# Start-up of an attention and gated-MLP kernel: the norm's scale on GpSimd, two tiles ahead, and the first Q and K loads ahead of the next weights

## The chip, the core and the metric

One core of one Trainium2 chip runs the kernel. The metric is the device time of one execution in microseconds (us). The engines are named as the profile names them: PE is TensorE (PEld is its loading of weights), DVE is VectorE, ACT is ScalarE, POOL is GpSimd and SP is SyncE, which issues most of the DMAs. An engine runs its instructions in the order in which they are written, and waits in that order too.

## What is computed

The reference, cut to what matters (S = 2048 tokens, D = 576, 32 heads of 18, 4608 hidden units, all f32):

```python
xn = layernorm(x)                                  # no gain, no bias
q, k, v = heads(xn @ wqkv)                         # 32 heads of 18
p = softmax(q @ k.T * 18 ** -0.5)                  # per head, 2048 x 2048
s = merge(p @ v) @ wo
h = gelu(xn @ w_gate) * (xn @ w_up)                # 2048 x 4608
return x + s * silu(h @ w_down)
```

The kernel holds every f32 operand of a matmul as two f16 parts, a high half and a low half (the rest), and multiplies high by high, high by low and low by high.

## The kernel before

**Order.** The function `tile_block_kernel` writes the program out in an order made by hand and by small planners. It has a start-up and a long main part. From about 220 us to the end the main part mixes the attention of all heads with the GLU matmuls, and its order is made by queues of pieces of work (`subtick`, `fill`, `g_run`) that are spent between matmuls.

**Norm.** `x` lies in SBUF as 16 tiles `xt[:, st]` of 128 tokens x 576. Per group of tiles `ln_stats` writes, on DVE, two `bn_stats` a tile (L1114) and one `bn_aggr` a tile (L1117), then for the group a square root on ACT (L1126), a reciprocal (L1127) and three small operations with two operands (L1120) that give the factor `rs_all`. The groups are tiles 0-1, 2-3, 4-7, 8-11 and 12-15. `ln_norm(st)` then subtracts the mean and multiplies by the factor, in place, on DVE (L1135, a `tensor_scalar` with two operands of one value per partition, `mv` and `rs_all`). ACT rounds to the high half `xn` (L1139), and POOL subtracts for the low half in two pieces, 64 columns (L1140) and 512 columns (L1141).

**Transposition and projection.** `ln_tr` puts nine 128x128 transpositions of a tile on PE (L1147) into a PSUM tile `tp`, and `ln_out` copies them on ACT to `XHT` (high, L1152) and `XL` (low, L1153). `proj_fine(st)` multiplies a tile by the Q and K weights of the first seven heads (28 matmuls, L412 to L415). After each fourth tile (a block of 512 tokens, `sb` 0 to 3) `evac_j` writes high and low halves of Q and K (ACT L514, DVE L519) and stores them to DRAM (L534), `QD` over POOL's DMA queue and `KD` over SP's. In the loop over `it` tile `it` is normalized, tile `it - 1` transposed, tile `it - 2` copied out and then projected.

**Weights.** `prep` makes one set of weights: the load (L229, L233, SP), row maxima (L248, DVE) and their exchange over DRAM (L274, L289, SP) for a common scale, a high half on ACT (L330) and a low half. The low half (`low`, L332) is one DVE instruction (L335) where `urgent` or `vec` is set, and two POOL instructions (L337 scale with one operand per partition, L338 subtract) elsewhere. `w0` are the Q and K weights of the first seven heads, `preps[0]` the V weights, whose pieces go into the loop by the table `V_PLAN` (iteration: pieces). After the loop `start_prep(1)` and `start_prep(2)` issue the loads of the Q and K weights of the next seven heads (`raw_j`) and line up the pieces of those and of GLU chunk 0 (`raw_c`).

**First scores.** Then `load_qk(0)` issues the loads of `KT` (L1242) and `QT` (L1243) of the first two heads from `KD` and `QD`, all on SP, and `fills(9, 2.0)` writes some 150 V matmuls (`unit_v`, L487 to L492, evacuated at L598 and stored to `VS` by POOL at L612). Only then come the first score matmuls `qk1(0, k)` (L1259), whose row maxima DVE takes (L1262, `PM`), two steps of `k` at a time between further V matmuls.

Of the kernel before, what the change touches and what calls it, by code (L numbers as in the profile page):

```python
# [31 lines left out]
V_PLAN = {8: 2, 9: 2, 10: 1, 11: 1, 12: 6, 13: 3, 14: 2, 15: 2, 16: 2, 17: 2}  # L32
# [62 lines left out]
def kernel(ctx: ExitStack, tc: tile.TileContext, x, wqkv, wo, w_gate, w_up, w_down, out):  # L95
# [114 lines left out]
    def prep(name, parts, n, down=None, urgent=False, free=None, dfree=None, lead=1, vec=()):  # L210
# [121 lines left out]
        def low(lo, raw, sc, hi, vec=False):  # L332

            if urgent or vec:
                nc.vector.scalar_tensor_tensor(lo, raw, sc, hi, op0=ALU.mult, op1=ALU.subtract)  # L335
            else:
                nc.gpsimd.tensor_scalar(raw, raw, sc, None, op0=ALU.mult)  # L337
                nc.gpsimd.tensor_tensor(lo, raw, hi, op=ALU.subtract)  # L338

        def split_lo(t):  # L340
            low(w.lo[:, t], w.raw[:, t], w.s[:, 0:1], w.hi[:, t], t in vec)
# [165 lines left out]
    def evac_j(j, part, sb, mt, n, late=None):  # L507
# [16 lines left out]
        def store():  # L524
# [7 lines left out]
            q = nc.gpsimd if j == 0 and part == 0 else nc.sync  # L532
# [459 lines left out]
    def start_prep(i):  # L992
        if i < len(order) and i not in preps:
# [4 lines left out]
                lead=2 if i == 3 else 1, vec=(1, 3) if i == 3 else (),  # L998
# [89 lines left out]
    w0, p0 = prep(*spec_j(0), urgent=True)  # L1088
# [44 lines left out]
    def ln_norm(st):  # L1133
        xs = xt[:, st]
        nc.vector.tensor_scalar(  # L1135
            xs, xs, mv[:, st, 0:1], rs_all[:, st:st + 1], op0=ALU.subtract, op1=ALU.mult
        )
        xn = xns[st] = ap.tile([P, 2 * D], F16, tag="P", name=f"xn{st}", bufs=6)
        nc.scalar.activation(xn[:, 0:D], xs, AF.Copy)  # L1139
        nc.gpsimd.tensor_tensor(xn[:, 576:640], xs[:, 512:576], xn[:, 512:576], op=ALU.subtract)  # L1140
        nc.gpsimd.tensor_tensor(xn[:, 640:1152], xs[:, 0:512], xn[:, 0:512], op=ALU.subtract)  # L1141

    def ln_tr(st):
        tp = tps[st] = ps.tile([P, 2, 1024], F16, tag=("s1", "s2")[st % 2], name=f"tp{st}")
        for i in range(9):
            b, c = divmod(i, 5)
            nc.tensor.transpose(tp[:, b, P * c:P * c + P], xns[st][:, P * i:P * i + P], ident)  # L1147

    def ln_out(st):
        sl = slice(P * st, P * st + P)  # L1150
        tp = tps[st]
        nc.scalar.activation(XHT[:, :, sl], tp[:, 0, 0:640].rearrange("p (a b) -> p a b", a=5), AF.Copy)  # L1152
        nc.scalar.activation(XL[:, :, sl], tp[:, 1, 0:512].rearrange("p (a b) -> p a b", a=4), AF.Copy)  # L1153
# [17 lines left out]
    with tc.manual_schedule():  # L1171
# [7 lines left out]
        s0, s1 = ln_stats(0, 2), ln_stats(2, 2)  # L1179
        for f in s0:  # L1180
            f()
        ln_norm(0)
        ln_norm(1)
        for f in s1[:3] + pw[:5]:
            f()
        ln_tr(0)
        ln_out(0)
        for f in pw[5:6] + s1[3:7] + pw[6:12] + s1[7:]:
            f()
        ln_norm(2)  # L1190
        pw[12]()
        ln_tr(1)
        ln_out(1)
        for f in pw[13:]:
            f()
        lnq = deque()
        for t in range(4, NT, 4):
            lnq.extend(ln_stats(t, 4))
        for _ in range(12):
            lnq.popleft()()  # L1200
        for it in range(2, NT + 2):
            g, i = divmod(it, 4)
            if 2 < it < NT:
                ln_norm(it)
            if g < 3:
                for _ in range((0, 0, 0, 5)[it] if it < 4 else (5, 4, 4, 4)[i]):
                    if lnq:
                        lnq.popleft()()
            if it == 5:
                open_j(w0, 0)  # L1210
            if it == 5:
                preps[0], pieces = prep(*order[0][1], urgent=True)
                pv0 = deque(f for _, f in pieces)
                pv0.popleft()()
            for _ in range(V_PLAN.get(it, 0)):
                pv0.popleft()()
            if it == 2:
                proj_fine(0)
            if it > 2:
                if it - 1 < NT:  # L1220
                    ln_tr(it - 1)
                if it - 2 > 1:
                    ln_out(it - 2)
                subtick()
                proj_fine(it - 2)
        while pv0:
            pv0.popleft()()
        start_prep(1)
        start_prep(2)
# [204 lines left out]
    load_qk(0)  # L1434
    fills(9, 2.0)
# [330 lines left out]
```

## Time and profile before

| what | us |
|---|---|
| median of the runs shown (2611.22 to 2614.23) | 2613.34 |
| the profiled execution's own time | 2613.96 |
| its span in the profile | 2612.2 |
| PE busy, share of the span | 2511.1, 96% |
| POOL busy, share of the span | 1507.7, 58% |

The profiled execution is 0.6 us above the median, and its span is 1.8 us shorter than its own time. Engines, their busy time and their share are in the page's first part; idle time of an engine that is not waited for costs nothing. The start-up is read by stages: a table of windows gives the busy time of each engine in each stretch, the granted TensorE clock and the DMA share, and the timelines of single engines give each instruction with the time it waited ahead of it, in brackets, and what ended the wait.

### The profile page before, as it was taken

To read this page: it belongs to the slowest core of one execution; us is meant where nothing else is said; L and a number is where in the kernel's file an instruction comes from. 1 tells how busy PE (TensorE), PEld (TensorE's weight loads), DVE (VectorE), ACT (ScalarE), POOL (GpSimd) and SP (SyncE) were. 2 spreads that over 40 slices of the span, in tenths; PEclk is the share of its full clock that TensorE was granted. 3 is DMA by queue.
4 is the path that set the end of the run, shared out by engine and by line. 5 is a ranking of instruction groups with operands and counts; after the bars stand their busy time and mean duration, and the time that the engine had idled before them with its cause. 6 is when DMAs were issued, how large, how long until landed. Compare 5 with 4: busy or idle time off the path is not lost. (4 is left out here: it accounts for less than half of the span.)

```text
span 2612.2 us, 60772 instructions
## 1 busy us (share of the span) xinstructions
PE 2511.1 (96%) x25800; PEld 1325.6 (51%) x25800; DVE 1931.7 (74%) x2713; ACT 1660.6 (64%) x2081; POOL 1507.7 (58%) x1426
## 2 busy tenths in 40 slices
PE   6899999999999999999999999999999999999997
PEld 5564545455545545455555455555445444445554
DVE  7587778777877777777777778777777777777544
ACT  5225666666767666766666666767666675766663
POOL 4247663576537553757656574847666675747412
PEclk9999999999999999999999999999999999999999
DMA  4431022202130112101011110201110111100123
GB/s 142 125 111 19 12 57 60 56 18 54 33 80 19 33 31 64 46 23 51 13 53 22 27 55 11 56 9 38 28 36 26 37 29 40 36 21 6 43 74 123
DMA packets 134156, 118.68 MB, mean 45 GB/s; under 512 B 60160, under 2 KB 112792, under 8 KB 133884
## 3 DMA queue, kind: packets, MB, share of 16 engines
q1 hardware_dynamic: 128892, 105.38, 15.2%
q0 software_dynamic: 2432, 6.54, 0.7%
q8 instruction: 201, 3.29, 0.5%
q10 hardware_dynamic: 2560, 2.89, 0.3%
q14 instruction: 71, 0.58, 0.1%
HBM read 84.89 MB, written 29.61 MB: 44 GB/s over the span
## 5 line engine op out<-in xcount | busy, mean ns | idle before, releaser
L1262 DVE TENSOR_REDUCE PM<-s 128x2 f32<-128x1024 f32 x1024 | 1250.9, 1224 | 341.5 <-PE s L1259 333.0
L1317 ACT ACTIVATE P<-s,etab 128x1024 f32<-128x1024 f32 x896 | 995.6, 1112 | 616.7 <-PE s L1311 601.1
L468 PE MATMUL ma_t<-XHT,whi_c 64*128 64x512 f16 x1440 | 542.9, 377 | 10.7 <-DVE osb L1342 5.6
L468 PE MATMUL mb_t<-XHT,whi_c 64*128 64x512 f16 x1440 | 542.9, 377 | 3.8 <-DVE touch L436 2.0
L468 PE MATMUL ma_t<-XHT,wlo_c 64*128 64x512 f16 x1296 | 488.5, 377 | 0.0
L468 PE MATMUL mb_t<-XHT,wlo_c 64*128 64x512 f16 x1152 | 434.1, 377 | 0.0
L468 PE MATMUL ma_t<-XL,whi_c 64*128 64x512 f16 x1152 | 433.8, 377 | 0.0
L468 PE MATMUL mb_t<-XL,whi_c 64*128 64x512 f16 x1152 | 433.7, 376 | 0.0
L1259 PE MATMUL s<-KT,QT 54*128 54x512 f16 x2048 | 399.5, 378 | 21.0 <-DMA QT<-QD 9.6
L1311 PE MATMUL s<-QT,KT 56*128 56x512 f16 x2048 | 406.0, 380 | 5.2 <-ACT P L1317 1.7
L468 PEld LDWEIGHTS <-whi_c 64*128 64x128 f16 x5184 | 276.8, 94 | 245.8 <-issue 30.4
L728 PE MATMUL md_t<-dhi_c,hhi 64*128 64x288 f16 x2304 | 341.7, 283 | 7.3 <-DVE osb L1344 2.3
L728 PE MATMUL md_t<-dhi_c,hlo 64*128 64x288 f16 x2304 | 341.4, 282 | 0.0
L728 PE MATMUL md_t<-dlo_c,hhi 64*128 64x288 f16 x2304 | 340.9, 282 | 0.0
L669 POOL TENSOR_SCALAR tw<-tw 128x512 f32<-128x512 f32 x144 | 90.9, 632 | 408.3 <-ACT tw L662 408.1
L728 PEld LDWEIGHTS <-hhi 64*128 64x128 f16 x4608 | 247.1, 94 | 141.4 <-issue 22.8
L1336 PE MATMUL md_t<-P,VT 128*32 128x512 f32 x2480 | 292.8, 596 | 0.7 <-ACT P L1317 0.5
L691 POOL TENSOR_TENSOR hlo<-gv,hhi 128x512 f16<-128x512 f32 x144 | 168.0, 1167 | 205.6 <-ACT hhi L684 194.9
L1311 PEld LDWEIGHTS <-KT 56*128 56x128 f16 x2048 | 126.0, 94 | 244.7 <-issue 158.4
L656 POOL TENSOR_TENSOR tw<-gs 128x512 f32<-128x512 f32 x144 | 150.6, 1046 | 140.1 <-ACT gs L633 139.7
L748 DVE SCALAR_TENSOR_TENSOR y<-md_t,c_c,y 128x576 f32<-128x576 f32 x272 | 219.2, 806 | 8.3 <-PE md_t L728 8.2
L468 PEld LDWEIGHTS <-wlo_c 64*128 64x128 f16 x2592 | 139.6, 94 | 122.1 <-issue 1.5
(249 smaller groups left out, 4067.2 us busy)
## 6 DMA issues: line engine op xcount, KB each, us to landing
draw_c<-in_B_w_down SPq DMA_DIRECT2D x18, 576.0 KB
raw_c<-in_B_w_gate SPq DMA_DIRECT2D x18, 512.0 KB
raw_c<-in_B_w_up SPq DMA_DIRECT2D x18, 512.0 KB
obr<-rd SPq DMA_DIRECT2D x30, 256.0 KB
KT<-KD SPq DMA_DIRECT2D x32, 224.0 KB
QT<-QD SPq DMA_DIRECT2D x32, 216.0 KB
VS<-vst POOLq DMA_DIRECT2D x16, 304.0 KB, 4.0
VT<-VS SPq DMA_DIRECT2D x16, 304.0 KB
```

What stands on the lines that cost most here:

```text
L468: nc.tensor.matmul(o, lw, xx, start=self.stage == 0 and self.k == 0, stop=self.stage == 1 and self.k == self.slots - 1, skip_group_check=True,
L656: gp.tensor_tensor(st["t"], st["g"], st["g"], op=ALU.mult)
L669: gp.tensor_scalar(st["t"], st["t"], 1.0, 1.0, op0=ALU.mult, op1=ALU.add)
L691: gp.tensor_tensor(hs.lo[:, ft], st["v"], hs.hi[:, ft], op=ALU.subtract)
L728: nc.tensor.matmul(self.t.t[:, hf, 0:288], a[r, ft, sl], b[r, ft, 288 * hf:288 * hf + 288], start=self.stage == 0 and k == 0, stop=self.st ...
L748: nc.vector.scalar_tensor_tensor(yy, y, w.c, yy, op0=ALU.mult, op1=ALU.add)
L1259: nc.tensor.matmul(s1[:, h], QT[p][r, P * qt:P * qt + P], KT[p][r, 512 * kb:512 * kb + 512], start=True, stop=True)
L1262: nc.vector.tensor_reduce(PM[p][:, :, qt, kb:kb + 1], s1, op=ALU.max, axis=AX.X)
L1311: nc.tensor.matmul(s2[:, h], KT[p][r, P * kt:P * kt + P], QT[p][r, 512 * qb:512 * qb + 512], start=True, stop=True)
L1317: nc.scalar.activation(pt, s2, AF.Exp, scale=ETAB[j0])
L1336: nc.tensor.matmul(t.t[qd:qd + 32, :], VT[p][:, c0:c0 + 32], pt[:, h], start=kt == k0, stop=kt == k1, skip_group_check=True,)
```

## The change

- **Scale on POOL.** `ln_norm` is split into `ln_scale` (the same `tensor_scalar`, now on GpSimd, L1135 of the new kernel), `ln_hi` (ACT, L1141) and `ln_lo` (one POOL instruction of 576 columns, L1145). In the loop at step `it` the scale of tile `it + 2` stands first, then the transpositions of tile `it`, the high half of `it + 1`, the copies of `it - 1`, the low half of `it + 1` and the projection of `it - 2`.
- **Statistics.** Groups are tiles 0-1, 2-3, 4-5, 6-7, 8-11 and 12-15, and they are written earlier.
- **Transpositions.** Ten a tile (L1151, L1153, L1155): four high, two of 64 columns, four low. The copies of the low half of tiles 9, 11, 13 and 15 go to DVE (L1163).
- **Weights.** The low halves 3 and 4 of `w0` go to POOL, 0 to 2 stay on DVE. Two of the low halves of each weight tile of GLU chunk 0 (`vec=(1, 3)`) go from POOL to DVE. `V_PLAN` spends the V pieces somewhat earlier.
- **Stores and loads.** The `QD` stores of the first three blocks go from POOL's to SP's queue. `start_prep(1)` and `start_prep(2)` stand behind `load_qk(0)`.

The order of PE's instructions from the seventh V matmul to the end is the same in both kernels (before, the first six stand between two projections), and so is that of the other engines from a little behind the first scores.

```diff
-V_PLAN = {8: 2, 9: 2, 10: 1, 11: 1, 12: 6, 13: 3, 14: 2, 15: 2, 16: 2, 17: 2}
+V_PLAN = {6: 2, 7: 2, 8: 1, 11: 1, 12: 6, 13: 3, 14: 3, 15: 3, 16: 2}
...
         def low(lo, raw, sc, hi, vec=False):
...
-            if urgent or vec:
+            if (urgent and vec is not None) or vec:
...
         def split_lo(t):
-            low(w.lo[:, t], w.raw[:, t], w.s[:, 0:1], w.hi[:, t], t in vec)
+            low(w.lo[:, t], w.raw[:, t], w.s[:, 0:1], w.hi[:, t], None if urgent and vec and t not in vec else t in vec)
...
-            q = nc.gpsimd if j == 0 and part == 0 else nc.sync
+            q = nc.gpsimd if j == 0 and part == 0 and sb == NB - 1 else nc.sync
...
-                lead=2 if i == 3 else 1, vec=(1, 3) if i == 3 else (),
+                lead=2 if i == 3 else 1, vec=(1, 3) if i in (2, 3) else (),
...
-    w0, p0 = prep(*spec_j(0), urgent=True)
+    w0, p0 = prep(*spec_j(0), urgent=True, vec=(0, 1, 2))
...
-    def ln_norm(st):
+    def ln_scale(st):
...
-        nc.vector.tensor_scalar(
+        nc.gpsimd.tensor_scalar(
...
-        xn = xns[st] = ap.tile([P, 2 * D], F16, tag="P", name=f"xn{st}", bufs=6)
-        nc.scalar.activation(xn[:, 0:D], xs, AF.Copy)
-        nc.gpsimd.tensor_tensor(xn[:, 576:640], xs[:, 512:576], xn[:, 512:576], op=ALU.subtract)
-        nc.gpsimd.tensor_tensor(xn[:, 640:1152], xs[:, 0:512], xn[:, 0:512], op=ALU.subtract)
+    def ln_hi(st):
+        xn = xns[st] = ap.tile([P, 2, D], F16, tag="P", name=f"xn{st}", bufs=6)
+        nc.scalar.activation(xn[:, 0], xt[:, st], AF.Copy)
+    def ln_lo(st):
+        xn = xns[st]
+        nc.gpsimd.tensor_tensor(xn[:, 1], xt[:, st], xn[:, 0], op=ALU.subtract)
...
     def ln_tr(st):
...
-        for i in range(9):
-            b, c = divmod(i, 5)
-            nc.tensor.transpose(tp[:, b, P * c:P * c + P], xns[st][:, P * i:P * i + P], ident)
+        xn = xns[st]
+        for c in range(4):
+            nc.tensor.transpose(tp[:, 0, P * c:P * c + P], xn[:, 0, P * c:P * c + P], ident)
+        for i in range(2):
+            nc.tensor.transpose(tp[64 * i:64 * i + 64, 0, 512:640], xn[:, i, 512:576], ident)
+        for c in range(4):
+            nc.tensor.transpose(tp[:, 1, P * c:P * c + P], xn[:, 1, P * c:P * c + P], ident)
...
     def ln_out(st):
...
+        lo = tp[:, 1, 0:512].rearrange("p (a b) -> p a b", a=4)
...
-        nc.scalar.activation(XL[:, :, sl], tp[:, 1, 0:512].rearrange("p (a b) -> p a b", a=4), AF.Copy)
+        if st >= 9 and st % 2:
+            nc.vector.tensor_copy(XL[:, :, sl], lo)
+        else:
+            nc.scalar.activation(XL[:, :, sl], lo, AF.Copy)
...
     def proj_fine(st):
...
+        early, late, high, low = pw[:5], pw[5:12], pw[12:13] + pw[13:20:2], pw[14:21:2] + pw[21:]
+        lnq = deque()
+        for t0, n in ((0, 2), (2, 2), (4, 2), (6, 2), (8, 4), (12, 4)):
+            lnq.append(deque(ln_stats(t0, n)))
+        def stats(n):
+            while n and lnq:
+                lnq[0].popleft()()
+                n -= 1
+                if not lnq[0]:
+                    lnq.popleft()
+        stats(11)
+        for t in range(2):
+            ln_scale(t)
+            ln_hi(t)
+        for t in range(2):
+            ln_lo(t)
+        stats(7)
+        for f in early[:4]:
...
+        stats(4)
+        early[4]()
...
+        for t in range(2, 4):
+            ln_scale(t)
+            ln_hi(t)
+        for t in range(2, 4):
+            ln_lo(t)
+        late[0]()
+        stats(3)
+        for f in late[1:]:
...
+        for f in high:
+            f()
+        stats(4)
+        for f in low[:3]:
+            f()
...
+        for f in low[3:]:
...
+        stats(4)
+        for t in range(4, 6):
+            ln_scale(t)
+        ln_hi(4)
         for it in range(2, NT + 2):
...
+            if it == 2:
...
+            stats(11 if it == 2 else 6)
+            if 5 < it + 2 < NT:
+                ln_scale(it + 2)
+            if it < NT:
+                ln_tr(it)
+            if 4 < it + 1 < NT:
+                ln_hi(it + 1)
+            if it - 1 < NT:
+                ln_out(it - 1)
+            if 3 < it + 1 < NT:
+                ln_lo(it + 1)
...
+            subtick()
+            proj_fine(it - 2)
...
-        start_prep(1)
-        start_prep(2)
...
+    start_prep(1)
+    start_prep(2)
```

**POOL, the norm loop.** The rows are of tiles 8 and 9 before, with the Q stores of the first block between them, and of tiles 0 to 7 in the new kernel. `xn_...` is the f16 tile of a norm tile, `evh` and `evl` the evacuated halves.

```order
L1140 TENSOR_TENSOR xn_530<-xt,xn_530 128x64
L1141 TENSOR_TENSOR xn_530<-xt,xn_530 128x512
L534 DMA QD_369<-evh_0_0_444 7x18x512 x2
L534 DMA QD_369<-evl_0_0_499 7x18x512
L1140 TENSOR_TENSOR xn_592<-xt,xn_592 128x64
L1141 TENSOR_TENSOR xn_592<-xt,xn_592 128x512
```

```order
L1145 TENSOR_TENSOR xn_171<-xt,xn_171 128x576
L1145 TENSOR_TENSOR xn_174<-xt,xn_174 128x576
L337 TENSOR_SCALAR raw_j_106<-raw_j_106,s_j_195 128x252
L338 TENSOR_TENSOR wlo_j_199<-raw_j_106,whi_j_198 128x252
L337 TENSOR_SCALAR raw_j_106<-raw_j_106,s_j_195 128x252
L338 TENSOR_TENSOR wlo_j_199<-raw_j_106,whi_j_198 128x252
L1135 TENSOR_SCALAR xt<-xt,mv,rs_all 128x576 x2
L1145 TENSOR_TENSOR xn_235<-xt,xn_235 128x576
L1135 TENSOR_SCALAR xt<-xt,mv,rs_all 128x576
L1145 TENSOR_TENSOR xn_374<-xt,xn_374 128x576
```

Before, POOL has one low half a tile and three stores a block; in the new kernel each tile brings a scale and a low half in turn, and two pairs of weight instructions stand ahead of tile 4.

**SP, the loads behind the norm loop.** `KD` and `QD` are the projected keys and queries in DRAM, `raw_j` the next weights, `mxd_j` their row maxima on the way to DRAM.

```order
L534 DMA KD_370<-evh_1_3_1052 7x18x512
L229 DMA raw_j_1066<-in_A_wqkv 128x4x126
L233 DMA raw_j_1066<-in_A_wqkv 128x1x126
L229 DMA raw_j_1066<-in_A_wqkv 128x4x126
L233 DMA raw_j_1066<-in_A_wqkv 128x1x126
L1242 DMA KT_1075<-KD_370 56x2048
L1243 DMA QT_1074<-QD_369 54x2048
L1242 DMA KT_1075<-KD_370 56x2048
L1243 DMA QT_1074<-QD_369 54x2048
L274 DMA mxd_j_1234<-mx_j_1232 128x1
```

```order
L534 DMA KD_238<-evh_1_3_1064 7x18x512
L1273 DMA KT_1082<-KD_238 56x2048
L1274 DMA QT_1081<-QD_237 54x2048
L1273 DMA KT_1082<-KD_238 56x2048
L1274 DMA QT_1081<-QD_237 54x2048
L229 DMA raw_j_1111<-in_A_wqkv 128x4x126
L233 DMA raw_j_1111<-in_A_wqkv 128x1x126
L229 DMA raw_j_1111<-in_A_wqkv 128x4x126
L233 DMA raw_j_1111<-in_A_wqkv 128x1x126
L274 DMA mxd_j_1320<-mx_j_1318 128x1
```

The four loads of the first two heads have passed the four loads of the next weights.

**DVE, the maxima behind the last evacuation.** `m_j` are the row maxima of the next weights, `PM` those of the scores `s`.

```order
L519 SCALAR_TENSOR_TENSOR evl_0_3_1058<-pv_t,evh_0_3_1054 126x512
L248 TENSOR_REDUCE m_j_1204<-raw_j_1066 128x1 x5
L262 TENSOR_REDUCE mx_j_1232<-m_j_1204 128x1
L1262 TENSOR_REDUCE PM_1080<-s_0_0_1276 128x2
L1262 TENSOR_REDUCE PM_1080<-s_0_1_1280 128x2
```

```order
L519 SCALAR_TENSOR_TENSOR evl_0_3_1070<-pv_t,evh_0_3_1066 126x512
L248 TENSOR_REDUCE m_j_1258<-raw_j_1111 128x1 x3
L1293 TENSOR_REDUCE PM_1087<-s_0_0_1282 128x2
L1293 TENSOR_REDUCE PM_1087<-s_0_1_1286 128x2
L248 TENSOR_REDUCE m_j_1258<-raw_j_1111 128x1 x2
L1293 TENSOR_REDUCE PM_1087<-s_0_2_1310 128x2
L1293 TENSOR_REDUCE PM_1087<-s_0_3_1314 128x2
L262 TENSOR_REDUCE mx_j_1318<-m_j_1258 128x1
```

Three of the five maxima of the next weights still stand ahead of the first row maxima, two come between them.

## Rows read from the trace of the kernel before

**Rows 1.** The page, first part: busy us (share of the span) and instructions of each engine.

```profile
PE 2511.1 (96%) x25800; PEld 1325.6 (51%) x25800; DVE 1931.7 (74%) x2713; ACT 1660.6 (64%) x2081; POOL 1507.7 (58%) x1426
```

**Rows 2.** Windows: stretch, its length, busy us of each engine (instructions), clock, DMA share.

```profile
core 0: us, PE busy (x) PEld busy (x) DVE busy (x) ACT busy (x) POOL busy (x), PEclk, DMA share, GB/s
24.00:62.00 38.00, 30.43 (x450) 28.42 (x448) 32.58 (x74) 27.54 (x50) 22.95 (x33) 0.96 0.25 74
...
85.00:95.00 10.00, 0.48 (x3) 0.20 (x4) 0.00 (x0) 0.00 (x0) 0.69 (x2) 0.69 0.21 44
95.00:100.00 5.00, 5.00 (x23) 2.34 (x24) 2.59 (x3) 0.41 (x1) 0.00 (x0) 0.60 0.55 120
100.00:105.00 5.00, 5.00 (x39) 3.16 (x37) 4.61 (x5) 0.82 (x2) 0.70 (x2) 1.00 0.44 138
```

**Rows 3.** PE's timeline: start us, us, operation, [idle before <-releaser].

```profile
67.52 0.29 PE L487 MATMUL ma_t<-whi_v,XHT 128*128 128x288 f16 x1
...
85.22 0.39 PE L1259 MATMUL s<-KT,QT 54*128 54x512 f16 x1 [0.27 <-DMA QT<-QD]
94.90 1.03 PE L1259 MATMUL s<-KT,QT 54*128 54x512 f16 x3 [9.29 <-DMA QT<-QD]
```

**Rows 4.** SP's timeline, issues of DMAs behind the norm loop.

```profile
70.00 0.96 SPq L229 DMA_DIRECT2D raw_j<-in_A_wqkv  x1
...
74.52 1.64 SPq L233 DMA_DIRECT2D raw_j<-in_A_wqkv  x1
76.34 2.06 SPq L1242 DMA_DIRECT2D KT<-KD  x1
...
79.38 0.47 SPq L1243 DMA_DIRECT2D QT<-QD  x1
```

**Rows 5.** DVE's timeline: the first scale, a small operation, the next weights' maxima, the first row maxima.

```profile
7.86 1.07 DVE L1135 TENSOR_SCALAR xt<-xt,mv,rs_all 128x576 f32<-128x576 f32 x2
...
25.95 1.08 DVE L1120 SCALAR_TENSOR_TENSOR nt<-mv,sd 128x4 f32<-128x4 f32 x1
27.06 0.16 DVE L1120 SCALAR_TENSOR_TENSOR nt<-nt,sd 128x4 f32<-128x4 f32 x1
...
81.94 1.38 DVE L248 TENSOR_REDUCE m_j<-raw_j 128x1 f32<-128x252 f32 x4 [12.90 <-DMA raw_j<-in_A_wqkv]
...
95.55 2.36 DVE L1262 TENSOR_REDUCE PM<-s 128x2 f32<-128x1024 f32 x2 [11.23 <-PE s L1259]
```

**Rows 6.** POOL's timeline: a low half, the last low half, the last Q stores.

```profile
25.86 1.15 POOL L1141 TENSOR_TENSOR xn<-xt,xn 128x512 f16<-128x512 f32 x1
...
60.80 1.15 POOL L1141 TENSOR_TENSOR xn<-xt,xn 128x512 f16<-128x512 f32 x1
...
69.98 0.61 POOL L534 DMA_DIRECT2D QD<-evl  x1
```

**Rows 7.** POOL's groups, whole run: xcount | busy us, mean ns | idle before.

```profile
L337 POOL TENSOR_SCALAR raw_c<-raw_c,s_c 128x512 f32<-128x512 f32 x88 | 139.3, 1583 | 60.8 <-ACT whi_c L330 51.9 <-PE s L1259 8.8
...
L669 POOL TENSOR_SCALAR tw<-tw 128x512 f32<-128x512 f32 x144 | 90.9, 632 | 408.3 <-ACT tw L662 408.1
...
L338 POOL TENSOR_TENSOR dlo_c<-draw_c,dhi_c 128x576 f16<-128x576 f32 x36 | 46.4, 1288 | 3.0
...
L337 POOL TENSOR_SCALAR raw_j<-raw_j,s_j 128x252 f32<-128x252 f32 x15 | 14.2, 948 | 7.6 <-ACT whi_j L330 7.5
L338 POOL TENSOR_TENSOR wlo_j<-raw_j,whi_j 128x252 f16<-128x252 f32 x15 | 10.0, 664 | 1.3
...
L337 POOL TENSOR_SCALAR raw_wo<-raw_wo,s_wo 128x576 f32<-128x576 f32 x5 | 8.6, 1722 | 0.0
```

**Rows 8.** DVE's groups, 0 to 66 us, same columns.

```profile
L1135 DVE TENSOR_SCALAR xt<-xt,mv,rs_all 128x576 f32<-128x576 f32 x16 | 11.7, 736 | 0.1
L335 DVE SCALAR_TENSOR_TENSOR wlo_v<-raw_v,s_v,whi_v 128x576 f16<-128x576 f32 x5 | 6.2, 1233 | 2.5 <-ACT whi_v L330 2.5
```

**Rows 9.** The page, DMA issues: KB each, median us from issue to landing.

```profile
VS<-vst POOLq DMA_DIRECT2D x16, 304.0 KB, 4.0
```

More of the change, by code (lines that the diff above doesn't have):

```diff
@@ L1178 @@
         pw = [f for _, f in p0[1:]]
-        s0, s1 = ln_stats(0, 2), ln_stats(2, 2)
-        for f in s0:
-            f()
[L1182 to L1185, printed above, removed]
+        early, late, high, low = pw[:5], pw[5:12], pw[12:13] + pw[13:20:2], pw[14:21:2] + pw[21:]
[16 more added lines that the diff above has]
+        for f in early[:4]:
+            f()
+        stats(4)
+        early[4]()
         ln_tr(0)
         ln_out(0)
-        for f in pw[5:6] + s1[3:7] + pw[6:12] + s1[7:]:
-            f()
-        ln_norm(2)
-        pw[12]()
+        for t in range(2, 4):
[6 more added lines that the diff above has]
+        for f in late[1:]:
+            f()
+        for f in high:
[3 more added lines that the diff above has]
+            f()
         ln_tr(1)
         ln_out(1)
-        for f in pw[13:]:
+        for f in low[3:]:
             f()
[L1196 to L1200, printed above, removed]
-        for it in range(2, NT + 2):
[L1202 to L1209, printed above, removed]
+        stats(4)
+        for t in range(4, 6):
+            ln_scale(t)
+        ln_hi(4)
+        for it in range(2, NT + 2):
+            if it == 2:
                 open_j(w0, 0)
-            if it == 5:
                 preps[0], pieces = prep(*order[0][1], urgent=True)
@@ L1214 @@
                 pv0.popleft()()
+            stats(11 if it == 2 else 6)
[9 more added lines that the diff above has]
+                ln_lo(it + 1)
             for _ in range(V_PLAN.get(it, 0)):
                 pv0.popleft()()
[L1217 to L1225, printed above, removed]
+            subtick()
+            proj_fine(it - 2)
         while pv0:
             pv0.popleft()()
-        start_prep(1)
-        start_prep(2)
         for _ in range(3):
```

## The prediction, as put on record ahead of the result

> **What bounds the kernel now.** I read the page's first part, then a table of windows over the start-up, then the timelines of PE, SP, DVE and POOL around the two stretches in which PE isn't full. PE is busy in 96% of the span [rows 1], and from the first scores on its order is the same in both kernels. So only the start-up can change, and the change is worth what it moves the point at which PE begins its unbroken run. Three things set that point.
>
> First, the norm loop. From 24 to 62 us DVE is busy 32.6 of 38 us and POOL 23.0, PE 30.4 [rows 2]: DVE sets the pace, with the statistics, the scales, the weights and the evacuations. The last low half of POOL ends at 60.80 + 1.15 = 61.95 [rows 6], and the block of V matmuls starts at 67.52 [rows 3]. That is a tail of 5.6 us for the transpositions and projections of the last tiles. Six V matmuls stand earlier, between two projections; in the new kernel they stand in the block.
>
> Second, the wait for Q and K. The V block lasts until the scores of the first head at 85.22; those of the second start at 94.90. PE waits 0.27 + 9.29 = 9.6 us, both times for the load of QT [rows 3]. SP explains it: the four loads of the next weights take from 70.00 to 76.16, then come KT and QT, the last one issued until 79.85 [rows 4].
>
> Third, the clock. From 85 to 95 us PE does three matmuls, and the granted clock is 0.69 over the stretch; from 95 to 100 it is 0.60, and PE, busy all the time, gets through 23 matmuls where the next 5 us bring 39 at clock 1.00 [rows 2]. The lost work is 16 of 39 matmuls, 16/39 x 5 = 2.1 us.
>
> Together second and third cost 9.6 + 2.1 = 11.7 us. If nothing else moved, that would be the whole gain.
>
> **The scale on POOL.** It takes 16 instructions of 0.74 us from DVE, 11.7 us of busy time [rows 8], and gives them to POOL, which already does the low halves. No row shows a POOL `tensor_scalar` with two operands of one value per partition. The nearest are those with one such operand: 1.72 us for 128x576 f32 [rows 7], the same shape. With constants only, 128x512 takes 0.63 us [rows 7], which is 0.71 for 576 columns. So one such operand costs (1.583 - 0.632) x 576/512 = 1.07 us by the rows of 512 columns. If the second costs as much as the first, a scale takes 2.79 us; if such an operand is read at the price of a constant here, 0.71. I take 1.72, the row of the same shape and type, and keep 0.71 and 2.79 as ends.
>
> The Trainium skill, "GPSIMD Engine Reference", 4.1 Engine selection, speaks for the low end: it has one-input operations on GpSimd at roughly line rate, and two-input ones at about twice DVE's time. The row of 1.72 us against DVE's 0.74 for the same shape says otherwise for an operand per partition; by the page the scale would take about the 0.74 of DVE, which is the rival "cheap" below.
>
> POOL's chain in the new kernel is then, from 7.86, where the first scale starts today [rows 5]: 16 scales x 1.72 = 27.5; 16 low halves in one piece at the 1.29 of the subtract of that shape [rows 7] = 20.6; and two low halves of `w0` at 0.95 + 0.66 [rows 7] = 3.2. That is 51.3 us, so POOL can't end before 59.2. It doesn't run without gaps. POOL and DVE hold each other up: the small operation at 25.95 took 1.08 us and ended with the low half that POOL had begun at 25.86, while the next of its kind took 0.16 [rows 5, 6]. In the new kernel POOL is nearly always running, so it will also find DVE first at times. DVE's two-operand instructions in the stretch are 18 small ones of 0.16 (2.9 us) and eight weight low halves of up to 1.2 [rows 5, 8], of which perhaps half the time falls on POOL; with waits for the statistics of tiles 0 to 7 I take 5 us, between 0 and 9. The last low half then ends at 59.2 + 5 = 64.2.
>
> The Trainium skill, "SBUF — State Buffer", Who interferes with whom, gives the rule: a DVE instruction with two SBUF inputs and a GpSimd instruction that reads SBUF exclude one another, and the later waits for the whole of the other. The trace agrees (1.08 us against 0.16).
>
> The tail behind the last low half is as today, 5.6 us, so the V block starts at about 69.8. Today it starts at 67.52, or 67.52 - 0.7 = 66.8 with the six earlier matmuls put into it: 141 matmuls take 85.22 - 0.27 - 67.52 = 17.4 us [rows 3], 0.12 each, six are 0.7. The loop gets **3.0 us longer**. DVE, relieved, doesn't help: the pace is now POOL's.
>
> **Loads of Q and K.** They no longer wait for 6.2 us of issues of the next weights. In the new kernel the last Q stores are issued about as long behind the start of the V block as today (69.98 + 0.61 against 67.52, 3.1 us) [rows 3, 6]. QT needs them landed; POOL's V stores take 4.0 us for that [rows 9], so at about 7 us the first QT can go and by about 8 us into the block all four loads are issued. The next weights were there 5.8 us behind their last issue (76.16 to 81.94) [rows 4, 5]; with 5 to 7 us Q and K are there 13 to 15 us into the block. The scores need them 17.4 + 0.7 = 18.1 us into the block. So 3 to 5 us are in hand, and the wait of 9.6 us and the low clock behind it, 2.1 us, go. PE then runs from the V matmuls into the scores without a break.
>
> **What is late next.** The loads of the next weights. Today their first issue is at 70.00 and the maxima of four of the five pieces start at 81.94 [rows 4, 5], 11.9 us later. In the new kernel they are issued from 8 us on, and DVE takes three of the five maxima ahead of the first row maximum. At today's pace the data would be there 20 us into the block, about 2 us behind the first scores; issued behind a nearly empty queue, sooner. PE has V matmuls to do meanwhile. I charge for the maxima that now stand among the row maxima, two of 0.35 us (1.38 / 4) [rows 5], **0.7 us**; DVE is at 4.6 of 5 us there [rows 2], so this delay reaches PE.
>
> **The rest.** Ten transpositions for nine, in a stretch where PE isn't full: nothing; without that cover one more is under 0.1 us a tile. The three blocks of Q stores on SP, which has little to do there: nothing, and POOL is spared their issue. Four copies of low halves on DVE, relieved of 11.7 us: nothing. Two low halves of GLU chunk 0 from POOL to DVE: they fall among the row maxima, where DVE is nearly full, but at most a few instructions of 0.75 to 1.2; the scores and GLU work are in PE's unchanged order, and I take 0, between -1 and +2. The earlier pieces of the V weights: nothing, they aren't last.
>
> **The sum.** +3.0 - 9.6 - 2.1 + 0.7 = -8.0 us against the profiled execution's own 2613.96, which is 2606.0; that execution lies 0.6 above the median, so **2605.4 us**.
>
> **The rivals.**
>
> *The scale costs 2.79 us* (slower). The second operand per partition then costs as much as the first. For it: the step from 0.71 to 1.72 by the first. Against: the instruction makes one pass over the same elements, and its price needn't add up. POOL's chain grows by 16 x 1.07 = 17.1 us, all on the path, so -8.0 + 17.1 = +9.1: 2622.5. It decides from 8.0 / 16 = 0.50 us on, a scale of 2.2 us; between 1.9 and 2.2 the result is within the noise. The Q and K loads are still in time, only everything is later.
>
> *The wait moves to the next weights.* The first row maximum stands behind three maxima of `raw_j`. For it: DMA moved almost nothing in the ten idle microseconds (a share of 0.21) [rows 2], and yet QT had been issued by 79.85 and came at 94.90, 15 us later; that slowness may not belong to the order of the loads at all. Against: the score tiles and the V matmuls behind them give PE some 2 us of cover, and the maxima needed `raw_j` for 11.9 us only. If the loads stall as QT did, the weights come 8 + 15 = 23 us into the block, DVE starts 5 us late, PE stands for some 3 to 4 us and its clock falls again, 2.1 us: -8.0 + 5.6 = -2.4, about 2611.
>
> *Cheap.* At 0.71 a scale POOL's chain is 16 us shorter, and DVE and PE bind. PE is busy 30.4 of 38 us [rows 2], so the loop can't give all of it; I take the block to start 6 us earlier than today instead of 3 later: -8.0 - 9 = -17, 2596.4.
>
> *The price lies between,* 1.9 to 2.3: 2609 to 2614.
>
> **How the numbers follow.** Forecast 0.46, cheap 0.09, the price between 0.13, the wait on the next weights 0.15, the scale at 2.79 0.17. What a measurement here can tell from no change is about 0.2%, 5.2 us. Faster than that, under 2608.1: forecast and cheap, less a little of the forecast's own upper end, 0.53. Within it: the price between and the moved wait, 0.30. Slower: the expensive scale, 0.17. The range leaves out the expensive scale and reaches from the cheap one to the price between with its gaps: 2596 to 2616. The forecast's own range, with gaps of 0 to 9 us in POOL's chain, is 2600 to 2610.
>
> **What would show it.** In the profile of the changed kernel: the mean of the scale on POOL (1.7, with 0.7 and 2.8 as the rivals); POOL busy in most of 8 to 64 us; the V block starting near 69.8; no wait for QT ahead of the scores and a granted clock of 1.00 through them; and DVE's wait for `raw_j` ahead of its first maxima ending before the scores. A V block that starts behind 78 would mean that the scale has eaten the gain; PE idle with DVE waiting for `raw_j`, that the wait has only moved. It is wrong altogether if the time changes by more than these shifts, for PE's later order is the same.

## The result, and the profile after

The changed kernel takes 2620.56 us (median of 8 runs, 2619.42 to 2623.76) against 2613.35 for the kernel before: a ratio of 1.0032, with a 95% interval of 1.0022 to 1.0042. It is **slower by 0.3%**, where I had forecast 2605.4 us and a range of 2596 to 2616. The profiled execution took 2620.3 us, its span is 2618.5.

First the scale on GpSimd. These are GpSimd's groups of the changed kernel, the answer to [rows 7] (count | busy us, mean ns | idle before):

```profile
L1135 POOL TENSOR_SCALAR xt<-xt,mv,rs_all 128x576 f32<-128x576 f32 x16 | 36.5, 2285 | 7.2 <-DVE rs_all L1120 7.2
...
L1145 POOL TENSOR_TENSOR xn<-xt,xn 128x576 f16<-128x576 f32 x16 | 20.3, 1274 | 0.0
```

A scale takes 2.285 us, not 1.72. The windows, as in [rows 2], show what this does to the norm loop, and what follows behind the V block:

```profile
core 0: us, PE busy (x) PEld busy (x) DVE busy (x) ACT busy (x) POOL busy (x), PEclk, DMA share, GB/s
...
24.00:62.00 38.00, 29.87 (x394) 26.18 (x393) 21.05 (x64) 20.42 (x38) 37.92 (x23) 1.00 0.28 86
...
95.00:100.00 5.00, 1.19 (x8) 0.36 (x6) 3.88 (x8) 0.00 (x0) 0.00 (x0) 0.96 0.09 27
100.00:105.00 5.00, 5.00 (x28) 3.00 (x29) 3.47 (x5) 0.53 (x2) 0.71 (x2) 0.69 0.18 62
```

GpSimd is busy 37.9 of 38 us, DVE only 21.1: the bound has moved from one to the other. From 95 to 100 us PE is nearly idle again (1.2 of 5 us), and behind it the granted clock is 0.69 over 5 us, with 0.50, the lower of its two levels (1.2 against 2.4 GHz), from 100 to 102 us. PE's timeline of the changed kernel, as in [rows 3], with its longest waits up to 190 us:

```profile
74.64 0.29 PE L487 MATMUL ma_t<-whi_v,XHT 128*128 128x288 f16 x1
...
92.74 0.60 PE L1290 MATMUL s<-KT,QT 54*128 54x512 f16 x4
...
98.36 0.39 PE L1290 MATMUL s<-KT,QT 54*128 54x512 f16 x2 [3.07 <-DVE PM L1293]
99.49 0.50 PE L1290 MATMUL s<-KT,QT 54*128 54x512 f16 x2 [0.74 <-DVE PM L1293]
...
157.06 0.37 PE L468 MATMUL mb_t<-XHT,whi_j 64*126 64x512 f16 x1 [2.15 <-DVE touch L436]
...
183.75 0.37 PE L468 MATMUL pv_t<-XHT,whi_j 64*126 64x512 f16 x1 [2.45 <-DVE touch L436]
```

The V block starts at 74.64. The scores follow at 92.74, both heads, without a wait for QT. But PE then waits 3.8 us for row maxima, and later twice more than 2 us. DVE's timeline says why:

```profile
96.11 1.06 DVE L248 TENSOR_REDUCE m_j<-raw_j 128x1 f32<-128x252 f32 x3 [19.37 <-DMA raw_j<-in_A_wqkv]
97.09 2.35 DVE L1293 TENSOR_REDUCE PM<-s 128x2 f32<-128x1024 f32 x2
...
156.21 0.74 DVE L253 TENSOR_REDUCE m_c<-draw_c 128x1 f32<-128x576 f32 x1
156.87 0.14 DVE L436 COPY touch<-mb_t 1x1 f32<-1x1 f32 x1
...
180.68 0.74 DVE L335 SCALAR_TENSOR_TENSOR wlo_c<-raw_c,s_c,whi_c 128x512 f16<-128x512 f32 x1
181.34 1.22 DVE L1293 TENSOR_REDUCE PM<-s 128x2 f32<-128x1024 f32 x1
182.47 1.17 DVE L335 SCALAR_TENSOR_TENSOR wlo_c<-raw_c,s_c,whi_c 128x512 f16<-128x512 f32 x1
183.56 0.14 DVE L436 COPY touch<-pv_t 1x1 f32<-1x1 f32 x1
```

DVE stood 19.37 us in front of the next weights' maxima, and the row maxima, for which PE waits, stood behind these. PE waits later for a `touch`, a copy of one element that DVE makes of the PSUM tile which PE writes next. At 156.87 it stands behind the weight maxima of GLU chunk 0 (before, at 154.69, directly behind a row maximum), at 183.56 behind two low halves of that chunk.

The balance of the two profiled executions. The second column says how much later the same instruction starts in the changed kernel, the third what was added since the line above:

| place | shift, us | added, us | where from |
|---|---|---|---|
| start of the V block, 74.64 against 66.8 | +7.8 | +7.8 | the scale on GpSimd |
| no wait for QT, no low clock behind it | | -11.7 | 9.6 + 2.1, as predicted |
| 25th row maximum | +2.2 | +6.1 | waits of 3.8 and 0.6 us for row maxima; 28 matmuls for 39 in 5 us, 1.4 us (5.8 in all) |
| 61st row maximum, 196.50 against 188.67 | +7.8 | +5.6 | waits of 2.15, 1.17 and 2.45 us for 1.03, 0.64 and 0.69 before, and two stretches of low clock behind them |
| last row maximum | +6.8 | -1.0 | the main part, both ways |

### The profile page after: what moved, and what is told of

Same layout as the page of the kernel before. It is cut to its first block, busy times and chain, and to the rows that moved or that the text cites. A ratio compares the mean times of both kernels' runs of the same rounds, so it can differ in the third digit from the quotient of the medians.

```text
span 2618.5 us, 60799 instructions
## 1 busy us (share of the span) xinstructions
PE 2516.0 (96%) x25816; PEld 1327.4 (51%) x25816; DVE 1921.2 (73%) x2705; ACT 1660.4 (63%) x2080; POOL 1533.4 (59%) x1417
```

## The experiments

All kernels but two were timed beside the kernel before (2612.2 to 2613.2 us); the two that only price an instruction ran once, for their profile.

### 1. The order of the loads undone

In the changed kernel:

```diff
     load_qk(0)
-    start_prep(1)
-    start_prep(2)
...
         while pv0:
             pv0.popleft()()
+        start_prep(1)
+        start_prep(2)
```

> The changed kernel (2620.6 us) with one part undone: the next weights are prepared ahead of the first Q and K loads again. The V block should still start at about 74.6 us, since the norm loop is untouched. Theory: the moved loads took away the wait for QT (9.6 us and 2.1 us of low clock) but brought the wait of the row maxima on raw_j (3.8 us and some 1.9 us of low clock), and, by putting every later piece of the weights' preparation further back in the program, the two long waits at 154 to 187 us (together some 5.6 us). Then the QT wait comes back and both others go: 2620.6 + 11.7 - 5.7 - 5.6 = about 2621. Rival: the waits at 154 to 187 us come from the two low halves of GLU chunk 0 on DVE; then they stay, and the time is about 2626. Second rival: the QT wait in the kernel before came from its V stores and weights in the DMA queues at that moment and doesn't return; then about 2609.

Measured: 2620.89 us (ratio 1.003, 1.0019 to 1.0041), the first theory's number. The wait for QT is back on PE's timeline of this kernel:

```profile
100.62 1.03 PE L1292 MATMUL s<-KT,QT 54*128 54x512 f16 x3 [7.77 <-DMA QT<-QD]
```

PE doesn't wait for row maxima there, and its waits from 160 to 192 us are 1.04, 0.64, 1.62, 0.69 and 0.69 us. So in this kernel moving the loads loses as much as it gains.

### 2. Chunk 0's low halves back on GpSimd

```diff
-                lead=2 if i == 3 else 1, vec=(1, 3) if i in (2, 3) else (),
+                lead=2 if i == 3 else 1, vec=(1, 3) if i == 3 else (),
```

> The changed kernel with only the two low halves of each GLU chunk 0 weight tile put back on GpSimd. Theory (the waits of 154 to 187 us come from the later place of the weights' preparation): the second wait there, 2.45 us behind two DVE low halves of 0.74 and 1.17 us, shrinks to about 0.7 and its low clock (about 2 us) goes, the first (2.15 us) stays: about 2617. Rival (all of it comes from these low halves): 2620.6 - 5.6 = 2615. Third: GpSimd then is late for the GLU pieces and the time is the same or longer, 2621 to 2624.

Measured: 2621.53 us (1.0033, 1.0021 to 1.0046), the third case. The wait of 2.45 us shrank to 0.69, as in the theory, and PE's timeline has a new one in its place:

```profile
191.45 0.39 PE L468 MATMUL ma_t<-XHT,wlo_c 64*128 64x512 f16 x1 [2.17 <-POOL wlo_c L338]
```

The first wait, 2.15 us, is untouched. With the preparation as late as it is, one of the two engines is late wherever these low halves stand.

### 3. The scale back on DVE

```diff
     def ln_scale(st):
...
-        nc.gpsimd.tensor_scalar(
+        nc.vector.tensor_scalar(
```

> The changed kernel with the scale of the norm on DVE again, at the new places in the order. Theory: the scale costs GpSimd 2.285 us each and makes GpSimd the bound of the norm loop; on DVE (0.74 us) the loop is bound by DVE and PE, and the V block starts at 60 to 67 us instead of 74.6; all that follows moves with it: 2606 to 2613. Rival: the end is set by when the loads land and not by when the V block starts, so that the wait on raw_j grows by what the loop saves: 2618 to 2621.

Measured: 2608.22 us (0.9979, 0.997 to 0.9987), within the theory's range and 12.3 us less than the changed kernel. PE's timeline and the windows of this kernel:

```profile
61.94 0.29 PE L487 MATMUL ma_t<-whi_v,XHT 128*128 128x288 f16 x1
```

```profile
24.00:50.00 26.00, 24.71 (x362) 22.06 (x360) 23.33 (x58) 19.63 (x37) 12.57 (x10) 1.00 0.34 107
```

The V block starts 12.7 us earlier, and PE is full from 24 us on (24.7 of 26 us). The waits of 2.15, 0.64, 1.16 and 2.45 us are still there, although `raw_j` lands 15 us earlier than in the changed kernel: they follow from what stands where in DVE's order, not from when data land. Between the 25th and the 61st row maximum they cost 2.2 us here, against 5.6 in the changed kernel. The waits have the same lengths, but no low clock stands behind them (1.00 from 156 to 162 us, against 0.72 in the changed kernel). So part of the 5.6 is clock, and that part doesn't come with every kernel.

The wait behind `raw_j` itself is down to 0.54 and 0.74 us, and one of 2.13 and 0.74 us has come further on. There DVE waits for the exchange of the maxima over DRAM, with row maxima behind it:

```profile
102.35 0.28 DVE L295 TENSOR_REDUCE mg_j<-mb_j 128x1 f32<-128x128 f32 x1 [2.28 <-DMA mb_j<-mxd_j]
```

```profile
104.58 0.39 PE L1290 MATMUL s<-KT,QT 54*128 54x512 f16 x2 [2.13 <-DVE PM L1293]
```

### 4. The loads first in the kernel before

The lines of the first experiment, the other way round, in the kernel before.

> The kernel before (2613.3 us) with one part of the change alone: the first Q and K loads ahead of the next weights. The V block should start at 67.5 us as before. Theory: the wait for QT goes (-11.7 us), the wait of the row maxima on raw_j comes (about +5.7), and the later place of the weights' preparation brings the waits behind the first scores (up to +5.6): 2607 to 2613. Rival (raw_j was late only because the changed kernel's norm loop pushed its V weights and stores late): no such waits, 2601.6.

Measured: 2610.40 us (0.9995, 0.9986 to 1.0004), no clear difference, within the theory's range. In the profile the 25th row maximum starts 5.8 us earlier than before, the 61st only 1.9 us. The wait for QT is gone; DVE waits 18.15 us for `raw_j`, PE 2.5 us for row maxima, then 2.15, 1.17 and, for GpSimd's low halves, 2.17 us.

### 5. The new norm loop alone

Both edits, the scale on DVE and the loads in their old order, in the changed kernel.

> The changed kernel with two parts undone: the scale of the norm on DVE and the next weights prepared ahead of the first Q and K loads. What is left is the new order of the norm loop. With the scale on DVE alone (2608.2 us) the V block started at 61.9 us, which should stay. Theory: the wait for QT comes back (some 8 to 10 us and 2 us of clock), the waits on raw_j and on the later preparation (about 8 us) go, so the two nearly cancel, as they did with the scale on GpSimd: 2607 to 2611. Rival: with an earlier V block the loads are in time in either order, and only the later preparation goes: 2601.

Measured: 2606.42 us (0.9974, 0.9964 to 0.9984), just under the theory's range; PE waits 6.10 us for QT, and the V block starts at 61.99. With this one the change falls into parts: the new order of the loop -6.8 us (2613.17 to 2606.42), the loads first +1.8 (to 2608.22), the scale on GpSimd +12.3 (to 2620.56). The +1.8 is within the noise: the two ratios, 0.9974 and 0.9979, lie in one another's intervals.

### 6. The next weights over another queue

In the kernel before, nothing moved in the program:

```diff
-        q = nc.sync
+        q = nc.scalar if name == "j1" else nc.sync
```

> The kernel before (2612.9 us) with one thing changed: the loads of the next seven heads' weights go over ACT's DMA queue, at the same place of the program, so that the first Q and K loads stand ahead of nothing of theirs on SP, and the preparation keeps its place. Theory: the wait for QT goes (-9.6 and -2.1 us of clock), no wait on raw_j and no waits of a later preparation come, ACT's four issues cost nothing: about 2601. Rival: QT is late because of what DMA moves at that time, whoever issues it; then the wait stays and the time is 2611 to 2614. It also tells whether the cost of the order in the changed kernel is its place in the program (then this one is faster than the loads-first version of the kernel before, 2610.4).

Measured: 2601.80 us (0.9956, 0.9942 to 0.9969). The same row maxima start 11.72 us earlier than in the kernel before, from the fifth to the 61st: the 9.6 + 2.1 us of the prediction, with nothing lost. The timelines of ACT's queue, SP's queue and PE in this kernel:

```profile
67.79 0.39 ACTq L229 DMA_DIRECT2D raw_j<-in_A_wqkv  x1
...
69.83 0.56 ACTq L233 DMA_DIRECT2D raw_j<-in_A_wqkv  x1
```

```profile
76.86 0.37 SPq L1242 DMA_DIRECT2D KT<-KD  x1
...
78.31 0.59 SPq L1243 DMA_DIRECT2D QT<-QD  x1
```

```profile
84.95 0.61 PE L1259 MATMUL s<-KT,QT 54*128 54x512 f16 x4
```

They correct my reason. The last load of QT is issued by 78.90, only 0.95 us earlier than the 79.85 of [rows 4], because SP now waits for the K stores to land before it issues KT; and yet QT is there for the scores, when before it came 15 us after its issue. The four issues ahead of it weren't what delayed QT.

What did is not shown. `raw_j` is on another queue here, but it is also issued earlier (67.79 to 70.39, against 70.00 to 76.16 before), and in every run with ACT's queue the two go together. In the kernel before, the QT of the first head, issued by 78.97 behind the same `raw_j`, was there at 85.22 [rows 3]. `raw_j` itself had landed when DVE began its last maximum at 83.71. PE waits on for the QT of the second head until 94.90, and from 88 us on DMA moves next to nothing; these are windows of the kernel before:

```profile
core 0: us, PE busy (x) PEld busy (x) DVE busy (x) ACT busy (x) POOL busy (x), PEclk, DMA share, GB/s
88.00:90.00 2.00, 0.00 (x0) 0.00 (x0) 0.00 (x0) 0.00 (x0) 0.00 (x0) 0.69 0.01 4
90.00:92.00 2.00, 0.00 (x0) 0.00 (x0) 0.00 (x0) 0.00 (x0) 0.00 (x0) 0.50 0.11 9
```

So neither the bulk of `raw_j` nor the load on DMA explains the last 7 us. SP's queue isn't the only late one either: the three V stores that POOL issues from 80 to 86 us take 12.8 us (median) to land before and 11.0 us in this kernel, against 4.0 over the whole run [rows 9]. Whether the queue itself or the earlier time of `raw_j` lets QT through stays open; a run with `raw_j` on ACT's queue at its old time would tell.

### 7. Scale on DVE, and the next weights over ACT's queue

> The changed kernel with the scale on DVE, the next weights prepared ahead of the first Q and K loads, and their loads over ACT's DMA queue: the parts that gained, without those that lost. Theory: V block at about 62 us, no wait for QT, none for raw_j, preparation in its old place: 2608.2 less some 8 us of waits and low clock behind the first scores = about 2600, or about 5 us earlier than the same edit on the kernel before. Rival: PE's earlier start only meets the same loads later on, 2605 to 2609.

Measured: 2597.47 us (0.9942, 0.9929 to 0.9954), 2.5 us under the forecast. PE waits neither for QT nor, at the first scores, for row maxima. Against the kernel of the fifth experiment only the queue of `raw_j` differs, and here the last load of QT is even issued 0.6 us later (by 74.11 against 73.51). There PE waited 6.10 us for it, until 86.58; here both heads' scores start at 80.60. So the time at which QT is issued isn't what makes it late.

### 8 and 9. What the scale's price depends on

In the changed kernel, by tile number modulo 3, with `a` and `b` per partition or constant:

```diff
+        a = mv[:, st, 0:1] if st % 3 < 2 else 0.03
+        b = rs_all[:, st:st + 1] if st % 3 == 0 else 1.02
+        nc.gpsimd.tensor_scalar(xs, xs, a, b, op0=ALU.subtract, op1=ALU.mult)
```

> The changed kernel with the scale on GpSimd in three forms, to price the operands: tiles 0, 3, 6, ... as they are (two operands of one value per partition), tiles 1, 4, 7, ... with a constant for the factor, tiles 2, 5, 8, ... with constants for both. The norm is wrong in two tiles of three; no work but these operands is left out. Theory: each operand per partition has its own price: 2.285 us, about 1.7 and 0.71. Rival: the first operand is dear and the second costs little or the two operations cost it: 2.285, 2.2 and 1.2.

Measured, in GpSimd's groups of this kernel; both theories fall:

```profile
L1137 POOL TENSOR_SCALAR xt<-xt,mv,rs_all 128x576 f32<-128x576 f32 x6 | 13.7, 2281 | 6.7 <-DVE rs_all L1120 6.6
...
L1137 POOL TENSOR_SCALAR xt<-xt,mv 128x576 f32<-128x576 f32 x5 | 11.0, 2209 | 0.0
L1137 POOL TENSOR_SCALAR xt<-xt 128x576 f32<-128x576 f32 x5 | 10.7, 2136 | 0.4
```

An operand per partition costs 0.07 us. The cheap row of 0.63 us in [rows 7] multiplies and then adds, the row of 1.72 only multiplies; so I priced the operations next:

```diff
+        if k == 0:
+            nc.gpsimd.tensor_scalar(xs, xs, b, a, op0=ALU.mult, op1=ALU.add)
+        elif k == 1:
+            nc.gpsimd.tensor_scalar(xs, xs, 1.02, 0.03, op0=ALU.mult, op1=ALU.add)
+        elif k == 2:
+            nc.gpsimd.tensor_scalar(xs, xs, 0.03, 1.02, op0=ALU.add, op1=ALU.mult)
+        else:
+            nc.gpsimd.tensor_scalar(xs, xs, 1.02, None, op0=ALU.mult)
```

> The changed kernel with the scale on GpSimd in four forms, to price the operations, since the operands cost only 0.07 us each: tiles 0, 4, ... multiply then add with two operands per partition, tiles 1, 5, ... multiply then add with constants, tiles 2, 6, ... add then multiply with constants, tiles 3, 7, ... one multiply with a constant. No tile is normalized as it should be; only these operands and operations differ. Theory: the pair multiply then add is the cheap form, as in the 0.63 us for 128x512 in the kernel before, and any other pair or a single operation is dear: 0.85, 0.71, 2.14 and 1.7 us. Rival: only the subtraction is dear: 0.85, 0.71, 0.71 and 0.7; the row of 1.72 us for a single multiply speaks against it.

Measured, in the same view; in the code lines 1139, 1141, 1143 and 1145 are the four forms in this order:

```profile
L1145 POOL TENSOR_SCALAR xt<-xt 128x576 f32<-128x576 f32 x4 | 6.6, 1650 | 0.1
...
L1139 POOL TENSOR_SCALAR xt<-xt,rs_all,mv 128x576 f32<-128x576 f32 x4 | 3.3, 817 | 6.7 <-DVE rs_all L1120 6.7
...
L1141 POOL TENSOR_SCALAR xt<-xt 128x576 f32<-128x576 f32 x4 | 2.7, 671 | 0.3
L1143 POOL TENSOR_SCALAR xt<-xt 128x576 f32<-128x576 f32 x4 | 2.7, 671 | 0.3
```

A multiplication and an addition, in either order, cost 0.67 us with constants and 0.82 with operands per partition. A lone multiplication costs 1.65, and subtract then multiply 2.14. The theory had the add-then-multiply form wrong (2.14 expected, 0.67 measured); the rival had the lone multiplication wrong.

### 10 to 12. The same scale as multiply and add

```diff
-            xs, xs, mv[:, st, 0:1], rs_all[:, st:st + 1], op0=ALU.subtract, op1=ALU.mult
+            xs, xs, rs_all[:, st:st + 1], nb_all[:, st:st + 1], op0=ALU.mult, op1=ALU.add
...
-            lambda: stt(r, c["t"], 1.5 * 2.0 ** 10, c["d"], ALU.add),
+            lambda: (
+                stt(r, c["t"], 1.5 * 2.0 ** 10, c["d"], ALU.add),
+                stt(nb_all[:, gs], mv[:, gs, 0], -1.0, r, ALU.mult),
+            ),
```

> The changed kernel with the same scale on GpSimd written as a multiplication by the factor and an addition of minus mean times factor, which costs one small DVE operation more a group. Theory: the scale takes 0.7 to 0.9 us, GpSimd no longer bounds the norm loop, the V block starts at about 62 us as with the scale on DVE, and the waits of the loads' order and of the later preparation stay: about 2608. Rival: a scale on GpSimd is dear in any form with operands per partition, 2.1 to 2.3 us: 2620.

Measured: 2604.03 us (0.9968, 0.9956 to 0.998), 16.5 us under the changed kernel. The scale takes 0.821 us and the V block starts at 62.23. The waits of 2.15 and 2.45 us are there to the hundredth. The median is 4 us under the theory's 2608 and the third experiment's 2608.22, but the intervals overlap, and of the two profiled executions this one is the slower (2606.87 against 2605.07), so a gain over the scale on DVE isn't shown.

With the loads over ACT's queue and in their old place as well:

> The last kernel with the next weights prepared ahead of the first Q and K loads and loaded over ACT's DMA queue. Theory: the V block starts where it does with the scale on DVE (62 us, PE is then full from 24 us on), so the time is that of the kernel with the scale on DVE and these loads: 2596 to 2599. If DVE was still a bound there, up to 2 us less; if the scale stays dear on GpSimd, about 2609.

Measured: 2595.11 us (0.9934, 0.9921 to 0.9947), a little under the theory's range and within the noise of the seventh experiment's 2597.47. And with the weights' own lone multiplication (L337) given an addition of zero:

```diff
-                nc.gpsimd.tensor_scalar(raw, raw, sc, None, op0=ALU.mult)
+                nc.gpsimd.tensor_scalar(raw, raw, sc, 0.0, op0=ALU.mult, op1=ALU.add)
```

> The last kernel (2595.1 us) with GpSimd's other single multiplication, the scale of the weights for their low halves, also written as a multiplication and an addition of zero. Theory: by the row of 0.67 us for constants and 0.82 with operands per partition, each of these 150 instructions falls from 1.6 or 1.75 to about 0.75 us, some 130 us of GpSimd's busy time, and the time hardly moves, because PE waits for GpSimd's low halves only 2.0 us in all, ahead of the first projections: 2592 to 2596. Rival: GpSimd's weight work delays DVE's or ACT's pieces in places that the waits don't name: more than 5 us faster, under 2590.

Measured: 2589.02 us (0.9907, 0.9891 to 0.9924), just on the rival's side, 3 us below the theory's range. This is the fastest kernel of the study. GpSimd's group, beside the row of 1583 in [rows 7]:

```profile
L337 POOL TENSOR_SCALAR raw_c<-raw_c,s_c 128x512 f32<-128x512 f32 x86 | 60.0, 698 | 65.3 <-ACT whi_c L330 56.5 <-PE s L1296 8.8
```

The first part of the page, of the kernel without this edit and of this one:

```profile
PE 2509.0 (97%) x25816; PEld 1324.9 (51%) x25816; DVE 1923.3 (74%) x2711; ACT 1661.2 (64%) x2080; POOL 1512.3 (58%) x1417
```

```profile
PE 2503.5 (97%) x25816; PEld 1322.7 (51%) x25816; DVE 1920.8 (74%) x2711; ACT 1661.3 (64%) x2080; POOL 1388.7 (54%) x1417
```

GpSimd has 123.6 us less to do, near the 130 of the theory. Against the kernel without this edit the same row maxima are 0.8 us earlier at the 61st, 4.6 at the 401st and 8.7 at the last: the gain is spread over the main part. The spans differ by 9.1 us (2594.2 and 2585.1), and 5.5 of them are PE's busy time, for the same number of matmuls. Most of that part is the clock. At three places behind 500 us it is low in the first execution and not in the second; one of them, first without and then with the edit:

```profile
733.00:739.00 6.00, 5.89 (x40) 2.86 (x41) 3.80 (x7) 1.53 (x3) 0.00 (x0) 0.72 0.24 69
```

```profile
730.00:736.00 6.00, 5.86 (x54) 3.11 (x55) 4.90 (x7) 2.54 (x5) 0.00 (x0) 1.00 0.24 69
```

In 6 us PE gets through 40 matmuls in the first and 54 in the second, and its wait just ahead is the same, 2.35 us in both. So this part doesn't come from a shorter wait there, and what is left for shorter waits is some 3.6 us. Whether the edit or chance kept the clock up isn't shown; the executions without the edit range from 2591.79 to 2602.41 us. That the instruction got cheaper is shown, that the 6 us between the medians come from it is not.

## Why the prediction was wrong, step by step

**The start of the V block** was put at 69.8 and came at 74.64. The step that failed is the price of the scale. I chose the row of the same shape, 1.72 us, and explained the difference to 0.63 by the operand per partition, at 1.07 us each. Such an operand measured 0.07. The dear thing is the operation, and that stands in the code beside the rows: the cheap instruction multiplies and adds, the one of 1.72 only multiplies, the scale subtracts first. At 2.285 us the term is 16 x 0.565 = 9.0 us larger. Part of this came back: I had allowed 5 us of gaps, and there were none (GpSimd's chain ran from 8.23 to 68.23 us, 60.0 us, against 36.5 + 20.3 + 3.3 = 60.1 of work), while the tail took 6.4 us for 5.6. 69.8 + 9.0 - 5.0 + 0.8 = 74.6. The low end of the bounds, 0.71, was near the price of another pair of operations: the multiply-and-add form took 0.82. There, as in the Trainium skill, "GPSIMD Engine Reference", 4.1 Engine selection, a one-input operation runs at roughly line rate (DVE took 0.74 us [rows 8]); the runs show that this holds for two forms of the instruction and not for the other two.

**The wait for QT and the clock** were right in size: 11.7 us, and the kernel before with the weights on ACT's queue gained 11.72. The reason given, the 6.2 us of issues, was not: the issue moved by 1 us in that kernel, and 0.6 us the wrong way in the seventh experiment against the fifth, and the wait was gone both times. So this term came out right by luck: QT went from late to in time by a mechanism that the prediction doesn't have and that these runs leave open.

**What is late next** had 0.7 us in the sum and measured about 5.8, which was the rival's 5.6. The step that failed is the cover. I counted 8 us to the first issue of `raw_j` and it was 85.08 - 74.64 = 10.4, since SP waited 5.1 us for the last K store ahead of KT, until 83.18, and 0.2 us for the last Q store ahead of QT; the 11.0 us from that issue to the first maximum at 96.11 were about the 11.9 that I had taken. And I let DVE's wait overlap with 2 us of V matmuls, while the row maxima stood behind three of its maxima from the first score on.

**The rest** had 0 for chunk 0's preparation, between -1 and +2, and measured +5.6. I looked at the loads that the two `start_prep` calls issue and not at the pieces that they line up. All of them, maxima, exchange and low halves, move back in DVE's, ACT's and GpSimd's order, where DVE is full. DVE's order is the same in both kernels only behind the low half at 182.47, some 90 us behind the first scores, and not from "a little behind" them, as the section on the change has it. The first, fourth and sixth experiments tell this from the other causes: with the old place the waits are short, with the new one the first of them is 2.15 us in all seven kernels that have it, whose loads landed at different times. Undoing only the low halves on DVE moved a wait to GpSimd. The size, 5.6, holds for this kernel: it has two stretches of low clock in it, and without them the same waits cost 2.2 us in the third experiment.

**The rivals.** The expensive scale gave 2622.5, near the result, for half the reason: the price was 2.285, just past the point of 2.2 from which it decides, and would have made +1.0 us alone. The moved wait came true beside it. I had given each a chance as if only one could happen. A sum over both, -8.0 + 9.0 + 5.1, is +6.1 and looks like the measured +7.2, but only because two errors that are left out nearly cancel, the gaps and the tail (-4.2) and the preparation (+5.6). With them it is +7.5.

## What to carry to other kernels

On GpSimd the price of `tensor_scalar` went with its operations more than with its operands: before an instruction is moved to another engine, its exact form is timed there, and a form with the same result may cost about a third (0.82 against 2.285 us). A load that is moved in the program takes with it everything that its preparation lines up on the other engines; a second queue moves the load alone (here 11 us faster, against 2.5 within the noise), though why QT then came in time these runs don't show. A difference of a few us between two profiled executions is first split into waits and clock. And when a wait is predicted to go, what then comes last on the same engine's queue is summed with the rest, not kept as a rival.

## What the hardware showed that I had not expected

GpSimd's `tensor_scalar` on 128x576 f32 took 0.67 us for multiply and add with constants, in either order, 0.82 with two operands per partition, 1.65 for a multiplication alone and 2.14 for subtract and multiply; each operand per partition added about 0.07. The QT of the second head, issued at nearly the same time, came 15 us after its issue with `raw_j` ahead of it on SP's queue and in under 7 us with `raw_j` on ACT's, while DMA was nearly idle (a share of 0.01 from 88 to 90 us) for part of the longer wait. And one and the same wait of PE, 2.35 us ahead of the same matmul, stood before a granted clock of 0.72 over 6 us in one execution and of 1.00 in another.
